# A stored order for 1,827 operations in the place of a list scheduler, in a complex linear attention with an expert layer

## The chip, the cores and the metric

One core of a Trainium2 chip runs the whole program. The metric is the device time of one execution in microseconds (us). Runs of the kernel before and of the changed kernel are compared on the same chip.

## The reference

The first half is a linear attention with a complex decay per channel, over 4 batches, 8 heads, 768 steps and 48 channels. The second half is an expert layer with 384 inputs and 2,048 hidden columns on all 3,072 tokens.

```python
mag = np.sqrt(a_re * a_re + a_im * a_im)
scale = np.minimum(mag, 0.999) / (mag + 1e-06)
a_re_n, a_im_n = (a_re * scale, a_im * scale)
for t in range(S):
    ar, ai = (a_re_n[:, :, t, :, None], a_im_n[:, :, t, :, None])
    new_re = ar * S_re - ai * S_im
    new_im = ar * S_im + ai * S_re
    kv = np.einsum('bhd,bhe->bhde', k[:, :, t], v[:, :, t])
    S_re, S_im = (new_re + kv, new_im)
    y[:, :, t] = np.einsum('bhd,bhde->bhe', q[:, :, t], S_re)
...
h = x @ w_in
g = h * (1.0 / (1.0 + np.exp(-1.702 * h)))
return (g @ w_out).astype(np.float32)
```

## The kernel before

The 3,072 tokens are cut into 12 units of 256 tokens (`u` 0 to 11). Each unit has two chunks of 128 tokens. Unit 0 is prepared in two halves of 128 tokens, so that the first matmuls can begin early.

`prepare` turns the decays into scaled and rotated queries and keys. It uses logarithms and exponentials on ScalarE (lines 569 to 581, one table), arctangent (line 589, another table), sine (lines 653 and 654, the table of the gate in all units but the first), and scans and products on VectorE. `remap` then moves `qr` and `qk` into the layout by heads, `qkh`, with five transfers from SyncE for each of the two (lines 676, 677, 679).

`attend` works on TensorE in four kinds of small pieces: the turning of keys (line 769), which ScalarE copies out to `kt` (line 772); the scores (line 714, 32 matmuls a piece), which VectorE multiplies by the mask into `pm` (line 718); the mix of scores, values and state (line 739), which ScalarE copies to `xhi` (line 748) and VectorE splits into `xlo` (line 752); and the update of the state (line 763). There is one PSUM tile for the scores, and one for the turned keys.

`moe` is the expert layer, over seven blocks of tokens: units 0 and 1 alone, in full fp32 (`whole`), and then five blocks of two units each, in three products of high and low halves. A hidden piece is line 819 (nine matmuls of 128x512 into `h_ps`, two buffers), the gate is line 832 on ScalarE (line 828 for the first two blocks), its split is lines 835 and 837 on VectorE, and a project piece is line 851 (nine matmuls, summed in three PSUM tiles `o_ps` over the block).

The weights arrive as 64-bit words. `convert` makes fp32 of them (lines 486 on ScalarE, 487, 490 and 493 on VectorE) and `split` makes the halves. Both lie in the first third of the program, beside the first units. Thirteen warm matmuls on data that are not used (line 661) run ahead of the first attention piece.

What sets the order is a planner. Every operation is an entry of `Plan` with its engine, an estimated duration, a rank, and the names of what it reads and writes. `Plan.order` ran a list scheduler forward and backward over the entries in many rounds, timed each candidate order with a model of the queues, and kept the best. Each engine then has the operations in the order so found, in one queue, and starts each when its inputs are there. Only the initial work stands outside of the plan: constants, the mask and the clearing of `qkh` (lines 393 to 412).

Of the kernel before, what the change touches and what calls it, by code (L numbers as in the profile page):

```python
# [21 lines left out]
P = 128  # L22
L = 128
HL = 64
QL = 32
NQ = L // QL
# [38 lines left out]
class Clock:  # L65


    def __init__(self):
        self.now, self.done, self.full = -1, 0.0, False

    def end(self, start, dur, work):
        t = start
        while dur > 1e-6:
            k = int(t / WINDOW + 1e-9)
            if k != self.now:
                self.full = k == self.now + 1 and self.done >= BUSY
                self.now, self.done = k, 0.0
            rate = 1.0 if self.full else 0.5
            step = min(dur, ((k + 1) * WINDOW - t) * rate)
            self.done += step * work  # L80
            dur -= step
            t += step / rate
        return t


def lag(a, b):
    return LAGS.get((a, b), LAG)


class Plan:  # L90
# [5 lines left out]
    def add(self, eng, dur, rank, fn, r=(), w=(), tab=None, name="", grp=None, work=1.0, kind=None):  # L96
# [10 lines left out]
        self.ops.append((eng, dur, rank, fn, deps, tab, name, grp, work))  # L107

    def link(self):
        self.after = [[] for _ in self.ops]  # L110
        for n, o in enumerate(self.ops):
            for d in o[4]:
                self.after[d].append(n)

    def groups(self):
        todo = {}
        for o in self.ops:
            if o[7] is not None:
                todo[o[7]] = todo.get(o[7], 0) + 1
        return todo  # L120

    def forward(self, rank, stay):

        ops, after = self.ops, self.after
        left = [len(o[4]) for o in ops]
        ready = [0.0] * len(ops)
        free = dict(FREE)
        wait = {e: [] for e in ENGINES}
        can = {e: [] for e in ENGINES}
        table, hw, dma, idle = None, 0.0, 0.0, 0.7  # L130
        todo, held = self.groups(), None
        clock = Clock()
        kinds, kind = self.kinds, "a"
        for n, k in enumerate(left):
            if not k:
                heapq.heappush(wait[ops[n][0]], (0.0, n))
        start = [0.0] * len(ops)
        done = 0
        while done < len(ops):
            best = None  # L140
            for e in ENGINES:
                while wait[e] and wait[e][0][0] <= free[e]:
                    n = heapq.heappop(wait[e])[1]
                    heapq.heappush(can[e], (rank[n], n))
                if can[e]:
                    s = free[e]
                elif wait[e]:
                    s = wait[e][0][0]
                else:
                    continue  # L150
                if best is None or s < best[0]:
                    best = (s, e)
            s, e = best
            if not can[e]:
                while wait[e] and wait[e][0][0] <= s:
                    n = heapq.heappop(wait[e])[1]
                    heapq.heappush(can[e], (rank[n], n))
            if e == "ACT":
                fit = [x for x in can[e] if ops[x[1]][5] in (None, table) or held in (None, ops[x[1]][7])]
                if not fit:  # L160
                    later = [free[x] for x in ENGINES if x != e and free[x] > s]
                    later += [wait[e][0][0]] if wait[e] else []
# [1051 lines left out]
```

## Time and profile before

| | us |
|---|---|
| median of 3 runs | 587.56 (585.82 to 588.19) |
| the profiled execution, its own time | 586.36 |
| its span | 584.6 |
| TensorE busy | 540.1 |
| VectorE busy | 470.1 |
| ScalarE busy | 275.6 |
| GpSimd busy | 27.4 |

The profiled execution lies 1.2 us under the median of the runs. Its span is what the profile shows from the first to the last instruction; 1.8 us of its time lie around the span. Busy time of TensorE counts overlapping matmuls once, and their ends are modelled.

### The profile page before, as it was taken

How to read it: one execution, taken by the hardware profiler on the slowest of the kernel's cores; microseconds unless marked ns; L12 is line 12 of the kernel's file. 1: busy time of each engine (PE TensorE's matmuls, PEld its weight loads, DVE VectorE, ACT ScalarE, POOL GpSimd, SP SyncE). 2: the span in 40 equal slices, each digit the busy share in tenths (PEclk: the TensorE clock that was granted, in tenths of full speed). 3: DMA queues.
4: the chain of work that ended last, by engine and by line, in shares of the span. 5: the costliest groups of instructions: out<-in, count | busy, mean ns of one | idle time of the engine just before them, and what ended most of it. 6: DMA issues, size and time to landing. Idle time of an engine off the chain costs nothing.

```text
span 584.6 us, 14786 instructions
## 1 busy us (share of the span) xinstructions
PE 540.1 (92%) x6236; PEld 445.1 (76%) x6236; DVE 470.1 (80%) x826; ACT 275.6 (47%) x428; POOL 27.4 (5%) x85
## 2 busy tenths in 40 slices
PE   0178999999999999999999999999999999999997
PEld 0166887887877878878888888878878888878885
DVE  6999889999899999888979789898775874654343
ACT  5975858885447355463543463553541221111110
POOL 7001000000101000000000000000000000000000
PEclk9998999999999999999999999999999999999999
DMA  8467983466455282681751762742962264232111
GB/s 323 138 193 304 275 259 117 82 193 116 164 137 166 44 169 72 116 267 51 138 181 44 148 214 69 135 171 69 185 192 73 66 119 82 85 127 56 36 46 56
DMA packets 30901, 80.06 MB, mean 137 GB/s; under 512 B 4208, under 2 KB 7024, under 8 KB 30832
## 3 DMA queue, kind: packets, MB, share of 16 engines
q1 hardware_dynamic: 30832, 79.09, 50.3%
q8 instruction: 49, 0.80, 0.6%
q14 instruction: 20, 0.16, 0.1%
HBM read 55.44 MB, written 4.72 MB: 103 GB/s over the span
## 4 chain that ended last, share of the span: by engine, by line
PE 66%; DVE 4%; issue 1%; ACT 1%; DMA 1%; DVEq 0%
PE o_ps L851 27%; PE h_ps L819 27%; PE x_ps L739 5%; PE p_ps L714 3%; PE kz_ps L769 2%; PE kz_ps L763 2%; DVE pm L718 1%; DMA raw_w<-in_w_in_dram 1%; DVE loU L511 0%; DVE qk L468 0%; DVE qr L468 0%; DVE gl L837 0%; DVE gh L835 0%; ACT kt L772 0%; DVE xlo L752 0%
## 5 line engine op out<-in xcount | busy, mean ns | idle before, releaser
L832 ACT ACTIVATE g<-h_ps 128x512 f32<-128x512 f32 x80 | 47.3, 597 | 161.3 <-PE h_ps L819 144.4
L851 PE MATMUL o_ps<-gh,hiU 128*128 128x512 f32 x240 | 96.5, 402 | 0.0
L819 PE MATMUL h_ps<-xhi,hiA 128*128 128x512 f32 x240 | 95.8, 399 | 0.6 <-ACT xhi L748 0.6
L851 PE MATMUL o_ps<-gl,hiU 128*128 128x512 f32 x240 | 93.8, 391 | 0.0
L819 PE MATMUL h_ps<-xlo,hiA 128*128 128x512 f32 x240 | 93.6, 390 | 0.1
L851 PE MATMUL o_ps<-gh,loU 128*128 128x512 f32 x240 | 93.6, 390 | 0.0
L819 PE MATMUL h_ps<-xhi,loA 128*128 128x512 f32 x240 | 93.6, 390 | 0.0
L835 DVE CAST gh<-g 128x512 fp32r<-128x512 f32 x80 | 33.8, 423 | 43.2 <-PE o_ps L851 39.3
L837 DVE TENSOR_TENSOR gl<-g,gh 128x512 fp32r<-128x512 f32 x80 | 55.2, 690 | 5.5
L772 ACT ACTIVATE kt<-kz_ps 128x224 f32<-128x224 f32 x80 | 28.3, 354 | 60.3 <-PE kz_ps L769 28.2
L819 PEld LDWEIGHTS h_ps<-xhi,hiA 128*128 128x128 f32 x240 | 45.0, 188 | 10.4 <-ACT xhi L748 0.9
L883 DVE TENSOR_REDUCE fit<-raw_w 128x1 f32<-128x256 f32 x96 | 37.8, 411 | 18.8 <-DMA raw_w<-in_w_out_dram 17.4
L851 PEld LDWEIGHTS o_ps<-gl,hiU 128*128 128x128 f32 x240 | 45.1, 188 | 10.2 <-DVE gl L837 0.6
L851 PEld LDWEIGHTS o_ps<-gh,hiU 128*128 128x128 f32 x240 | 45.1, 188 | 9.9 <-issue 1.0
L819 PEld LDWEIGHTS h_ps<-xhi,loA 128*128 128x128 f32 x240 | 45.1, 188 | 9.5
L819 PEld LDWEIGHTS h_ps<-xlo,hiA 128*128 128x128 f32 x240 | 45.1, 188 | 9.1 <-DVE xlo L752 0.4
L851 PEld LDWEIGHTS o_ps<-gh,loU 128*128 128x128 f32 x240 | 45.1, 188 | 8.4
L851 PE MATMUL o_ps<-g,valU 128*128 128x256 f32 x192 | 46.6, 383 | 1.6 <-issue 1.0
L819 PE MATMUL h_ps<-x,valA 128*128 128x256 f32 x192 | 47.7, 392 | 0.0
L468 DVE TENSOR_TENSOR qk<-qk,s 128x768 f32<-128x768 f32 (+1 forms) x52 | 45.3, 890 | 2.5 <-ACT s L654 1.8
L718 DVE TENSOR_TENSOR pm<-p_ps,mask 128x512 f32<-128x512 f32 x48 | 33.1, 690 | 15.7 <-PE p_ps L714 14.5
L1039 ACT ACT_TABLE_LOAD x35 | 44.9, 1283 | 1.4 <-PEq L1202 0.8
(92 smaller groups left out, 857.5 us busy)
## 6 DMA issues: line engine op xcount, KB each, us to landing
v<-in_v_dram SPq DMA_DIRECT2D x24, 416.0 KB, 3.9
ri<-in_a_dram SPq DMA_DIRECT2D x11, 768.0 KB, 5.2
qk<-in_qk_dram SPq DMA_DIRECT2D x11, 768.0 KB, 5.0
qkh<-qr SPq DMA_DIRECT2D x22, 288.6 KB, 5.8
qkh<-qk SPq DMA_DIRECT2D x22, 288.6 KB, 6.7
raw<-in_w_in_dram SPq DMA_DIRECT2D x8, 768.0 KB, 7.4
raw<-in_w_out_dram SPq DMA_DIRECT2D x8, 768.0 KB, 5.3
raw_w<-in_w_in_dram SPq DMA_DIRECT2D x24, 256.0 KB, 2.9
```

The source lines that it names most:

```text
L468: add(en, t, rank, lambda: e.tensor_tensor(out=out, in0=a, in1=b, op=alu), **kw)
L714: mm(p_ps[to : to + QL, j, lo:L], lhsT=at(h, 1, c)[:, lo : lo + QL], rhs=at(h, 0, c)[:, lo:L], start=True, stop=True)
L718: add("DVE", d_t(CW), rk(4 * c + hh), lambda hh=hh: dve.tensor_tensor(out=pm[hh], in0=p_ps, in1=mask, op=ALU.mult), r=["P"], w=[f"pm{hh}"])
L739: mm(x_ps[32 * j : 32 * j + 32, r, :], lhsT=lt, rhs=rt, start=n == 0, stop=n == len(steps) - 1)
L772: add("ACT", a_t(2 * KD) - 0.12, rk(4 * c + hh), lambda e=e: act(out=kt[0][:, 2 * e : 2 * e + 2, :], in_=k_ps, func=AF.Copy), r=["K"], w=[ ...
L819: mm(h_ps[hb][:, hs], lhsT=ww[:, r * T + f * P : r * T + (f + 1) * P], rhs=x[:, r, :], start=r + k == 0, stop=r == NR - 1 and k == len(ter ...
L832: add("ACT", a_t(N) - 0.15, rk(i + f / 2), lambda hb=hb, hs=hs: act(out=g32[hb][:, hs], in_=h_ps[hb][:, hs], func=AF.Silu, scale=SLOPE), r ...
L835: add("DVE", d_t(N, 2), rk(i + f / 2), lambda hb=hb, hs=hs: dve.tensor_copy(out=high.g(hb)[:, hs], in_=g32[hb][:, hs]), r=regs("g", kf), w ...
L837: add("DVE", d_t(N), rk(i + f / 2), lambda hb=hb, hs=hs: dve.tensor_tensor(out=glo[hb][:, hs], in0=g32[hb][:, hs], in1=high.g(hb)[:, hs].b ...
L851: mm(o_ps[m][:, 0:N], lhsT=y[:, f * DM + m * P : f * DM + (m + 1) * P], rhs=x[:, hs], start=i == 0 and f == 0 and k == 0, stop=i == NP - 1 ...
L883: add("DVE", d_t(CK), rk + 2, lambda x=x, op=op: dve.tensor_reduce(out=f_w[:, x, n : n + 1], in_=weights.looked_at()[:, :, 1], op=op, axis ...
L1039: nc.scalar.preload_act_table_set(o[5])
```

## The change

The list scheduler and its model go, with all their constants. `Plan.order` now reads a stored list of 1,827 numbers and asserts that it holds every operation once and each behind those that it depends on. The list was found by annealed moves inside the engines' queues. The operations themselves are the 1,819 of before and eight new ones. The eight are `clear`: the second `qkh` buffer was cleared by one GpSimd instruction of 4,104 columns ahead of the plan, and is now cleared by eight of 513 columns in the plan, which wait for the first `rc` of unit 0. The mask is made with six copies in place of twelve. The argument `size` on the entries is not read any more when the kernel is built.

```diff
     def order(self):
-
-        self.link()
-        best = None
-        for part, stay in PARTS:
-            rank = [o[2] for o in self.ops]
-            for k in range(ROUNDS):
-                start, end = self.forward(rank, stay)
-                order = sorted(range(len(start)), key=lambda n: start[n])
-                cost = sum(w * self.time(order, x) for x, w in COST)
-                if best is None or cost < best[0]:
-                    best = (cost, order)
-                late = self.backward(start)
-                rank = [x + part * (end - y - x) for x, y in zip(rank, late)]
-        return best[1]
+        coded = base64.b85decode("".join(ORDER))
+        order = struct.unpack(f">{len(coded) // 2}H", coded)
+        place = {n: i for i, n in enumerate(order)}
+        assert len(place) == len(self.ops) == len(order)
+        assert all(place[d] < place[n] for n, o in enumerate(self.ops) for d in o[4])
+        return order
...
+CLEAR = 513
+ORDER = (
+    "0D=He0002L0A&CV0I2{90G9xR0E7Th0EGaC08#*l08;>q0Ehro00IC30FM9z0FVGx0E_@u09gP80F3}z0FD4%0FwY)0A2uz09*iJ0Ez%t0FeM#"
...
-    for j in range(1, NQ):
-        for x in range(NQ):
-            y = (x + j) % NQ
-            nc.gpsimd.tensor_copy(out=mask[y * QL : (y + 1) * QL, j, :], in_=mask[x * QL : (x + 1) * QL, 0, :])
+    for x in range(NQ):
+        y = (x + 1) % NQ
+        nc.gpsimd.tensor_copy(out=mask[y * QL : (y + 1) * QL, 1, :], in_=mask[x * QL : (x + 1) * QL, 0, :])
+    for x in range(2):
+        nc.gpsimd.tensor_copy(out=mask[(1 - x) * HL : (2 - x) * HL, 2:NQ, :], in_=mask[x * HL : (x + 1) * HL, 0:2, :])
     half = H * T
     nc.vector.memset(qkh[0][:, 0:half], 0.0)
     nc.gpsimd.memset(qkh[0][:, half:], 0.0)
-    nc.gpsimd.memset(qkh[1], 0.0)
...
+    def clear(n):
+        part = qkh[1][:, n * CLEAR : min((n + 1) * CLEAR, H * (2 * T + 1))]
+        add("POOL", 0.45, 14 + 0.5 * n, lambda: pool.memset(part, 0.0), r=["rc0"], w=[f"H1.{c}.{x}" for c in range(2) for x in range(2)])
+
     for n, units in enumerate(BLOCKS):
+        if n == 1:
+            for k in range(-(-H * (2 * T + 1) // CLEAR)):
+                clear(k)
         for u in units:
             prepare(u)
             attend(u)
```

Three places show how the queues change. Lines 511, 536, 560 and 566 of the changed kernel are lines 714, 739, 763 and 769 of before; 616 and 648 are 819 and 851; 843 is 1039; 629 is 832; 366 and 367 are 569 and 570.

The first place is TensorE's queue at the second chunk of unit 8, before: two score pieces follow each other with only one turning of keys between them.

```order
L714 MATMUL p_ps<-qkh_76 32x128 x4
L714 MATMUL p_ps<-qkh_76 32x96 x4
L714 MATMUL p_ps<-qkh_76 32x64 x4
L714 MATMUL p_ps<-qkh_76 32x32 x4
L769 MATMUL kz_ps<-ident,qkh_76 128x112 x2
L714 MATMUL p_ps<-qkh_75 32x128 x4
L714 MATMUL p_ps<-qkh_75 32x96 x4
L714 MATMUL p_ps<-qkh_75 32x64 x4
```

The same score piece of chunk 1 of unit 8 now has a hidden piece of nine matmuls ahead of it.

```order
L566 MATMUL kz_ps<-ident,qkh_76 128x112 x2
L616 MATMUL h_ps_106<-xhi_2905,hiA_884 128x512
L616 MATMUL h_ps_106<-xlo_91,hiA_884 128x512
L616 MATMUL h_ps_106<-xhi_2905,loA_1860 128x512
L616 MATMUL h_ps_106<-xhi_2905,hiA_884 128x512
L616 MATMUL h_ps_106<-xlo_91,hiA_884 128x512
L616 MATMUL h_ps_106<-xhi_2905,loA_1860 128x512
L616 MATMUL h_ps_106<-xhi_2905,hiA_884 128x512
L616 MATMUL h_ps_106<-xlo_91,hiA_884 128x512
L616 MATMUL h_ps_106<-xhi_2905,loA_1860 128x512
L511 MATMUL p_ps<-qkh_76 32x128 x4
```

An update of the state and a project piece stand ahead of this turning, so that two pieces of nine matmuls now lie between the two score pieces of the chunk.

The second place is TensorE's queue where the last block of the expert layer begins, before: the first hidden piece stands right behind the last mix of unit 11.

```order
L739 MATMUL x_ps<-pm_95,v_87 32x128 x2
L739 MATMUL x_ps<-pm_96,v_87 32x128 x2
L739 MATMUL x_ps<-qkh_75,st_94 32x128 x4
L819 MATMUL h_ps_105<-xhi_4732,hiA_358 128x512
L819 MATMUL h_ps_105<-xlo_91,hiA_358 128x512
L819 MATMUL h_ps_105<-xhi_4732,loA_730 128x512
```

Now a project piece of the block before stands between that mix and the hidden piece.

```order
L536 MATMUL x_ps<-qkh_75,st_94 32x128 x4
L648 MATMUL o_ps_107<-gh_1724,hiU_1231 128x512
L648 MATMUL o_ps_107<-gh_1724,loU_2230 128x512
L648 MATMUL o_ps_107<-gl_100,hiU_1231 128x512
L648 MATMUL o_ps_108<-gh_1724,hiU_1231 128x512
L648 MATMUL o_ps_108<-gh_1724,loU_2230 128x512
L648 MATMUL o_ps_108<-gl_100,hiU_1231 128x512
L648 MATMUL o_ps_109<-gh_1724,hiU_1231 128x512
L648 MATMUL o_ps_109<-gh_1724,loU_2230 128x512
L648 MATMUL o_ps_109<-gl_100,hiU_1231 128x512
L616 MATMUL h_ps_105<-xhi_4754,hiA_1014 128x512
```

A project piece has moved in between the last mix of a unit and the first hidden piece of the next block; this is so at all five blocks of two units.

The third place is ScalarE's queue where unit 6 is prepared beside the expert block of units 2 and 3, before: all logarithms and exponentials of the unit (lines 569 to 581) stand between two table loads, and no gate among them.

```order
L1039 ACT_TABLE_LOAD
L569 ACTIVATE s_84<-s_84,small 128x3x256
L772 ACTIVATE kt_97<-kz_ps 128x224
L748 ACTIVATE xhi_1913<-x_ps 128x3x128
L570 ACTIVATE s_84<-s_84 128x3x256
L772 ACTIVATE kt_97<-kz_ps 128x224
L580 ACTIVATE s_80<-s_84,small 128x3x256
L581 ACTIVATE s_80<-s_80 128x3x256
L578 ACTIVATE s_81<-s_81,small 128x3x256
L579 ACTIVATE s_81<-s_81 128x3x256
L1039 ACT_TABLE_LOAD
```

Now, where unit 7 is prepared beside that same block, the logarithm and its exponential have a table load of their own, and the sine of unit 6 and the gates follow with another.

```order
L843 ACT_TABLE_LOAD
L366 ACTIVATE s_84<-s_84,small 128x3x256
L367 ACTIVATE s_84<-s_84 128x3x256
L843 ACT_TABLE_LOAD
L451 ACTIVATE s_85<-s_85 128x3x256
L629 ACTIVATE g_99<-h_ps_106 128x512
L569 ACTIVATE kt_97<-kz_ps 128x224
L629 ACTIVATE g_98<-h_ps_105 128x512
```

Gates have moved in between the parts of a unit's group of logarithms, with a table load at each change. In the whole queue the executed loads go from 35 to 59.

## Rows read from the trace of the kernel before

**Rows 1.** The page's part on engines, first line: busy us, share, instructions.

```profile
PE 540.1 (92%) x6236; PEld 445.1 (76%) x6236; DVE 470.1 (80%) x826; ACT 275.6 (47%) x428; POOL 27.4 (5%) x85
```

**Rows 2.** Busy time by stage: stretch, us, engines, granted clock, DMA share, GB/s.

```profile
0.00:49.93 49.93, 17.64 (x361) 14.40 (x361) 43.76 (x86) 35.85 (x58) 15.43 (x35) 1.00 0.68 241
49.93:140.00 90.07, 88.21 (x884) 75.43 (x882) 85.52 (x126) 66.37 (x104) 2.33 (x10) 0.98 0.66 185
140.00:300.00 160.00, 155.77 (x2025) 127.21 (x2017) 145.61 (x244) 85.81 (x127) 6.74 (x25) 1.00 0.55 136
300.00:514.00 214.00, 212.20 (x2690) 174.06 (x2688) 166.11 (x306) 77.90 (x125) 2.87 (x15) 1.00 0.47 118
514.00:580.40 66.40, 66.17 (x290) 53.96 (x290) 28.40 (x64) 9.62 (x17) 0.00 (x0) 1.00 0.19 57
```

**Rows 3.** Timeline of the opening: start, us, engine, line, operation, idle before.

```profile
8.91 3.52 POOL L410 MEMSET qkh<- 128x4104 f32 x1
...
9.99 2.86 DVE L487 TENSOR_SCALAR valA<-raw 128x768 int32<-128x768 int32 x1 [1.48 <-DMA raw<-in_w_in_dram]
...
26.60 7.44 PE L661 MATMUL h_ps<-qk,ident 128*128 128x256 f32 x26 [26.60 <-DVE qk L468]
...
28.33 1.17 SPq L676 DMA_DIRECT2D qkh<-qk  x2
...
31.62 0.55 DVE L487 TENSOR_SCALAR valA<-raw 128x768 int32<-128x768 int32 x1
...
33.88 0.36 PE L769 MATMUL kz_ps<-ident,qkh 112*128 112x112 f32 x2
...
35.99 0.34 ACT L772 ACTIVATE kt<-kz_ps 128x224 f32<-128x224 f32 x1
```

**Rows 4.** Timeline, end of unit 0's attention and the first hidden piece.

```profile
44.41 0.75 DVE L718 TENSOR_TENSOR pm<-p_ps,mask 128x512 f32<-128x512 f32 x1
...
46.78 2.08 DVE L628 TENSOR_TENSOR_SCAN s<-small,s 128x256 f32<-128x256 f32 x3
...
49.40 0.35 PE L763 MATMUL kz_ps<-v,kt 128*16 128x48 f32 x12 [2.41 <-issue]
...
49.93 7.04 PE L819 MATMUL h_ps<-x,valA 128*128 128x256 f32 x24
```

**Rows 5.** Busy time by stretch just behind it; the granted clock stands third from the end.

```profile
50.00:52.00 2.00, 2.00 (x7) 1.63 (x7) 2.00 (x4) 1.81 (x3) 0.00 (x0) 0.58 1.03 419
52.00:54.00 2.00, 2.00 (x6) 1.59 (x6) 2.00 (x4) 1.37 (x2) 0.00 (x0) 0.57 0.29 113
```

**Rows 6.** Timeline of TensorE, five of its waits; the bracket is idle before.

```profile
146.11 1.13 PE L851 MATMUL o_ps<-g,valU 128*128 128x256 f32 x4 [1.04 <-issue]
...
183.48 1.00 PE L714 MATMUL p_ps<-qkh 128*32 128x128 f32 x30 [0.84 <-DVE pm L718]
...
218.97 0.41 PE L769 MATMUL kz_ps<-ident,qkh 112*128 112x112 f32 x2 [1.13 <-ACT kt L772]
...
387.56 0.77 PE L714 MATMUL p_ps<-qkh 128*32 128x128 f32 x30 [0.49 <-DVE pm L718]
...
514.12 0.50 PE L819 MATMUL h_ps<-xhi,hiA 128*128 128x512 f32 x1 [0.61 <-ACT xhi L748]
```

**Rows 7.** Timeline of TensorE where a hidden piece ends and a mix follows.

```profile
295.11 0.39 PE L819 MATMUL h_ps<-xlo,hiA 128*128 128x512 f32 x1
295.33 0.39 PE L819 MATMUL h_ps<-xhi,loA 128*128 128x512 f32 x1
295.65 0.86 PE L739 MATMUL x_ps<-pm,v 128*32 128x128 f32 x24
```

**Rows 8.** Groups on ScalarE: count, busy us, mean ns, idle before, what ended it.

```profile
L832 ACT ACTIVATE g<-h_ps 128x512 f32<-128x512 f32 x80 | 47.3, 597 | 161.3 <-PE h_ps L819 144.4 <-DVE gl L837 7.8 <-issue 5.6
L1039 ACT ACT_TABLE_LOAD x35 | 44.9, 1283 | 1.4 <-PEq L1202 0.8
```

More of the change, by code (lines that the diff above doesn't have):

```diff
@@ L1 @@
-import heapq
+import base64
 import math
+import struct
 from contextlib import ExitStack
@@ L62 @@
 SLOPE = 1.702
[L65 to L87, printed above, removed]
 class Plan:
@@ L94, in __init__, with add @@
         self.ops, self.wrote, self.read, self.kinds = [], {}, {}, []
-    def add(self, eng, dur, rank, fn, r=(), w=(), tab=None, name="", grp=None, work=1.0, kind=None):
+    def add(self, eng, dur, rank, fn, r=(), w=(), tab=None, name="", grp=None, work=1.0, kind=None, size=1):
         n = len(self.ops)
@@ L282, in time @@
-    def time(self, order, load):
-        ops = self.ops
-        free = dict(FREE)
-        ends = [0.0] * len(ops)
-        table, hw, dma, idle = None, 0.0, 0.0, 0.7
-        clock = Clock()
-        kinds, kind = self.kinds, "a"
-        for n in order:
-            e, dur = ops[n][0], ops[n][1]
-            s = max([free[e]] + [ends[d] + lag(ops[d][0], e) for d in ops[n][4]])
-            if e == "SP":
-                free[e] = s + 0.06 + 0.65 * (ops[n][8] - 1)
-                hw = max(hw, s + 0.06) + 0.47 * ops[n][8]
-                dma = max(dma, hw + 0.6) + dur
-                ends[n] = dma + 0.9
-                continue
-            if ops[n][5] not in (None, table):
-                dur += max(0.0, load - (s - idle))
-                table = ops[n][5]
-            if e == "PE":
-                dur += CHANGE[kind, kinds[n]]
-                kind = kinds[n]
-            free[e] = ends[n] = clock.end(s, dur, ops[n][8]) if e == "PE" else s + dur
-            if e == "ACT":
-                idle = s + dur
-        return max(ends)
@@ L715, in scores @@
                                start=True, stop=True)
-                add("PE", 0.6, rk(4 * c + hh), scores, r=hk[c], w=["P"], name=f"P{u}.{c}.{hh}", work=0.97, kind="m")
+                add("PE", 0.6, rk(4 * c + hh), scores, r=hk[c], w=["P"], name=f"P{u}.{c}.{hh}", work=0.97, kind="m", size=4 * NQ * NQ + 1)
                 add("DVE", d_t(CW), rk(4 * c + hh), lambda hh=hh: dve.tensor_tensor(
@@ L823, in moe @@
                 for rs in PIECES:
-                    add("PE", len(rs) * terms_of * columns, rk(i + f / 2 - 0.5), lambda rs=rs, hidden=hidden: hidden(rs), r=xk + cols, w=regs("h", kf), name=f"H{n}.{i}", work=0.975, kind="a")
+                    add("PE", len(rs) * terms_of * columns, rk(i + f / 2 - 0.5), lambda rs=rs, hidden=hidden: hidden(rs), r=xk + cols, w=regs("h", kf), name=f"H{n}.{i}", work=0.975, kind="a", size=len(rs) * (4 if whole else 6) + 1)
             for f in range(2):
@@ L861, in moe @@
                     r=[k for y in (("gh",) if whole else ("gh", "gz")) for f in fs for k in regs(y, at(f)[2])] + cols, w=[f"o{m}" for m in ms],
-                    name=f"O{n}.{i}", work=0.975, kind="a")
+                    name=f"O{n}.{i}", work=0.975, kind="a", size=len(fs) * len(ms) * (4 if whole else 6) + 1)
         spent = [f"x{y}{b}.{c}" for y in "hl" for c in range(4)]
```

234 lines of the change are left out of this document (47 added, 187 removed).

## The prediction

> **What bounds the kernel now.** I read the page's line of engines first: TensorE is busy for 540.1 us of the span of 584.6, VectorE for 470.1, ScalarE for 275.6 [rows 1]. TensorE bounds, so the next question is where it does not work. The stages answer it [rows 2]. Up to 49.93 us, where the first hidden piece of the expert layer starts [rows 4], TensorE is busy for 17.64 us: this opening is bounded by VectorE (43.76 us busy of 49.93) and by what it feeds. From there to 580.4 us TensorE idles for 1.86, 4.23, 1.80 and 0.23 us in the four stages (stretch less busy), 8.12 us in all. In that second part a new order can only win these 8.12 us, a stretch at half clock, and the small cost of changing from one kind of matmul to another; the matmuls themselves stay.
>
> The idle 8.12 us come in a few large waits, and I looked each up. Five are in [rows 6]. The waits at 183.48 and 387.56 us are of a kind that comes at least twice more: a score piece stands right behind the one before it, and must wait until VectorE has read the single PSUM tile of scores. The wait at 218.97 us is a turning of keys behind ScalarE's copy of the last one. The wait at 514.12 us is the first hidden piece of the last block behind the copy of the mix. The wait at 146.11 us is of another sort: it begins in the middle of a piece and ends by "issue", so neither data nor a buffer was late; the queue had no instruction ready. The largest of this sort lies in the opening, 2.41 us in the middle of a state update [rows 4]. Behind it the first hidden pieces run at a granted clock of 0.58 and 0.57 for the next four microseconds [rows 5], nearly half of 2.4 GHz: some 4 x 0.42 = 1.7 us lost.
>
> **The change part by part.**
>
> *GpSimd's clearing.* One clearing of 3.52 us, from 8.91 to 12.43 us, overlaps a VectorE conversion that takes 2.86 us; the same conversion takes 0.55 us elsewhere [rows 3]. The conversion ends 0.42 us behind the clearing, so I read it as held up by it: 2.31 us of VectorE in the opening. The clearing now comes in eight pieces, 3.52 x 513 / 4,104 = 0.44 us each, so one conversion can be held up by that much at most. The pieces stand in the plan behind unit 0's first `rc`, and the buffer is first written by unit 2, so nothing waits for them. The fewer mask copies are hidden: nothing reads the mask before unit 0's scores.
>
> *The opening's order.* The second half of the decay work of unit 0 is now first, and one weight is converted between, with its load moved ahead of the queries' loads on SyncE. In time for the first attention piece it matters that SyncE's second five transfers, those from `qk`, start at 28.33 us [rows 3], though their input was complete when the warm matmuls started, at 26.60 us: SyncE was still issuing the five from `qr`. In the new VectorE queue the two products for `qr` stand well ahead of the last product for `qk`, with scans and products between, so the first five will be out when the second can start. That is worth up to 28.33 - 26.60 = 1.7 us; and five of the thirteen warm matmuls, which end just before the first turning at 33.88 us, are moved behind it. ScalarE's first copy of keys, at 35.99 us, is 2 us behind the turning that it copies [rows 3]; in the new queue it stands earlier against unit 1's logarithms. So the first attention pieces come 2 to 3 us earlier. But then a loss: in the new VectorE queue unit 1's angle scan (three instructions, 2.08 us, [rows 4]) stands ahead of the last mask product of unit 0, where before only a decay product and one conversion step stood, and three more conversion steps stand ahead of the mask product before that. I take 1.2 us for the opening: from 0 (all given back by VectorE, which has hardly a gap there) to 2.4 (the 2.41 us wait for instructions gone, and nothing else).
>
> *The half clock.* It came behind the wait for instructions. Three warm matmuls now stand between the second chunk's pieces, but a wait for the last mask product stays. I take half of 1.7 us, 0.8; bounds 0 and 1.7.
>
> *Waits in the second part.* I went through the new TensorE queue for the four kinds of wait. No score piece stands behind another any more without either an expert piece or mixes of the chunk between them; nine matmuls in steps of 0.22 to 0.23 us [rows 7] are 2.0 us, and the mask product that must fit in between takes 0.75 [rows 4]. Before every block of two units a project piece stands between the last mix and the first hidden piece, 2.0 us against the 0.61 that it idled. The turning of 218.97 us has three expert pieces ahead of it. So these waits go: the five of [rows 6] less that for instructions are 3.07 us, and two more of the score kind, which I take at 0.4 each since the two shown are 0.84 and 0.49, make it 3.9. The waits for instructions stand behind dense runs of small matmuls, which expert pieces now break up more evenly. I take another 1.2 us there, a little more than the one of 1.04, and leave 3.0 of the 8.12 as they are: a gain of 5.1. Bounds: 2 (VectorE's waits come back elsewhere) and 8.1.
>
> *Changes of kind.* A matmul step of 0.22 us inside a hidden piece becomes 0.32 us where a mix follows [rows 7]: 0.1 us for leaving, and I bound the entry by the same. TensorE's queue changes between expert and attention pieces 150 times before, and 140 times now: 1.0 us. Of the returns to expert work, 32 came directly from scores, mixes or updates and 15 do now; the others go by way of a turning of two matmuls. I take 1.5 us; bounds 0 and 2.5.
>
> *ScalarE's tables.* 24 more loads at 1.283 us are 30.8 us of ScalarE [rows 8]. It idles 161.3 us ahead of the 80 large gates alone, nearly all for TensorE [rows 8], and a load has no input to wait for, so it runs in such an idle stretch. I take nothing for it; if the cover is gone, a load delays the gate and then the project piece by up to 1.28 us. The Trainium skill speaks against this part: "ScalarE: Activation LUTs", section "What ACT_TABLE_LOAD costs", counts a drain of 1.38 us with each load, 2.66 us for every switch. By that figure the 24 loads would be an estimated 64 us of ScalarE, still less than its idle time. The trace of before agrees with the load's 1.283 us and shows 1.4 us of idle ahead of all 35 together, which leaves no room for a drain there.
>
> *The sum.* 1.2 + 0.8 + 5.1 + 1.5 = 8.6 us against the profiled execution's 586.36, so 577.8. The median of the runs is 1.2 us above that execution, and I set the forecast against the median: **579.0 us**, 1.5% faster. The likeliest case's own range is from 573 (nearly all of the idle time and the clock) to 584.
>
> **The rivals.** *VectorE keeps the time.* In the stage from 49.93 to 140 us VectorE is busy for 85.52 of 90.07 us, and from 140 to 300 us for 145.61 of 160 [rows 2]. If the gates' splits and weight halves are late whatever TensorE's order, waits move from score pieces to expert pieces. For it: only 4.6 us of VectorE's time are free in the first of these stages. Against it: by 300 us another 14.4 are, and the clearing gives 2.3 back. Then only the last 284 us gain (2 us of idle time) and about 1 us of changes: 584 to 587. *The order has nothing to give*, since it does not fit the chip and each of its wins is paid elsewhere: also here.
>
> *More is won.* The waits for instructions and the half clock go altogether, and the opening gains 2.4: 2.4 + 1.7 + 8.1 + 2.5 = 14.7, so 573 or less.
>
> *Slower, by ScalarE's tables.* In the stretches where a unit's logarithms are cut by gates, a gate has two loads, 2.57 us, and the logarithms' part between them ahead of it. If TensorE has fewer than two expert pieces of other work between that gate's hidden piece and its project piece, it waits. It decides from 8.6 / 1.283 = 7 exposed loads on; with all in twelve places exposed it is 15.4 us: 579 + 15.4 = 594. Against it: in the new queue I find a project piece only rarely less than two expert pieces behind its hidden piece. For it: it is the one thing of which the change adds much. The skill's rule to batch work by table set ("ScalarE: Activation LUTs", section "Table sets: the hidden batching unit") would make this rival the case.
>
> **How the numbers follow.** The forecast's case has 0.60, more won 0.10, VectorE or nothing to give 0.20, slower 0.10. What a measurement of this kernel tells from no change is about half a per cent, 584.6 to 590.5. The second rival lies across its lower edge, a quarter of it faster, and a little of the forecast's own case falls short of it too. So faster 0.74, within 0.17, slower 0.09. The range leaves out the far parts of the first and last cases: 570.5 to 588.
>
> **What the profile after would show.** Right: the conversion of line 487 near 9 us takes about 0.6 us; the first hidden piece starts between 47.5 and 50; no granted clock near 0.6 behind it; TensorE idles some 3 us from there on; 59 table loads, with the gates' idle time still mostly for TensorE. Wrong: waits of TensorE's expert pieces for `g`, `gl` or `lo`, which would be VectorE or ScalarE late; or a first hidden piece later than 51 us.

## The result, and the profile after

The changed kernel takes 579.19 us (median of 4 runs, 578.89 to 579.99); the kernel before took 587.88 in the runs beside it (4 runs, 585.82 to 589.58). The ratio is 0.9856, with a 95% interval of 0.9822 to 0.9889: faster by 1.4%. The forecast was 579.0. The profiled execution took 579.99 us, span 578.3, against 586.36 and 584.6.

The page of the changed kernel, its part on engines, and the group of table loads:

```profile
PE 535.9 (93%) x6236; PEld 442.3 (76%) x6236; DVE 462.3 (80%) x826; ACT 301.0 (52%) x452; POOL 29.8 (5%) x86
...
L843 ACT ACT_TABLE_LOAD x59 | 75.7, 1283 | 1.8 <-PEq L1006 0.8
```

Busy time by stage of the changed kernel, columns as in [rows 2]. The first stage now ends at the first hidden piece, 47.61 us, and the last with TensorE:

```profile
0.00:47.61 47.61, 17.97 (x361) 13.99 (x361) 43.33 (x87) 35.54 (x58) 9.78 (x30) 1.00 0.70 245
47.61:140.00 92.39, 88.20 (x965) 74.69 (x958) 87.55 (x130) 74.28 (x111) 11.19 (x19) 1.00 0.66 182
140.00:300.00 160.00, 158.15 (x2106) 130.69 (x2109) 145.18 (x245) 92.62 (x134) 5.45 (x23) 1.00 0.54 139
300.00:514.00 214.00, 213.90 (x2570) 175.85 (x2563) 161.02 (x307) 91.09 (x138) 3.34 (x15) 1.00 0.45 118
514.00:571.60 57.60, 57.59 (x255) 47.05 (x253) 24.52 (x58) 7.45 (x13) 0.00 (x0) 1.00 0.19 58
```

The span's 6.3 us have three parts. The first hidden piece is 2.3 us earlier (49.93 to 47.61). From there to the last matmul it is 523.99 us instead of 530.47, 6.5 less. But the span ends 6.7 us behind the last matmul (578.3 - 571.6), where before it ended 4.2 behind it (584.6 - 580.4): 2.5 us are given back.

What TensorE waits for, all stages together (total us, times, longest):

```profile
PE h_ps L616 <- ACT g L625: 4.6, 5, 1.5
PE x_ps L536 <- DVE pm L515: 1.8, 2, 1.2
PE kz_ps L560 <- DVE st L579: 1.6, 1, 1.6
PE p_ps L511 <- issue: 1.0, 1, 1.0
```

The waits of score pieces for the mask product, of the turning and of the last block's hidden piece [rows 6] are gone. The wait "by issue" of 1.04 us at 146.11 is gone too, but one of 0.95 us now stands in a score piece at 155.59 (the last line). The first line is new: hidden pieces that wait for a gate of the whole blocks. Here are TensorE's large waits in order of time:

```profile
39.04 0.53 PE L560 MATMUL kz_ps<-v,kt 128*32 128x48 f32 x32 [1.60 <-DVE st L579]
...
45.35 0.43 PE L536 MATMUL x_ps<-pm,v 128*32 128x128 f32 x8 [1.25 <-DVE pm L515]
...
60.71 1.56 PE L616 MATMUL h_ps<-x,valA 128*128 128x256 f32 x6 [0.97 <-ACT g L625]
...
106.46 2.86 PE L616 MATMUL h_ps<-x,valA 128*128 128x256 f32 x12 [0.62 <-ACT g L625]
...
110.79 1.56 PE L616 MATMUL h_ps<-x,valA 128*128 128x256 f32 x6 [1.48 <-ACT g L625]
...
118.60 1.56 PE L616 MATMUL h_ps<-x,valA 128*128 128x256 f32 x6 [0.86 <-ACT g L625]
...
146.36 1.56 PE L616 MATMUL h_ps<-x,valA 128*128 128x256 f32 x6 [0.68 <-ACT g L625]
...
155.59 0.34 PE L511 MATMUL p_ps<-qkh 128*32 128x64 f32 x10 [0.95 <-issue]
```

The timeline of ScalarE ahead of the wait at 118.60 shows why the gate is late: it stands behind an arctangent, a weight half that nobody needs soon, and a table load. A table load of 1.28 us stands right ahead of three of the five late gates (at 104.73, 116.87 and 144.63 us).

```profile
110.36 0.38 ACT L625 ACTIVATE g<-h_ps 128x256 f32<-128x256 f32 x1
...
113.98 1.28 ACT L843 ACT_TABLE_LOAD   x1
115.28 0.84 ACT L386 ACTIVATE s<-s 128x768 f32<-128x768 f32 x1
116.03 0.83 ACT L303 ACTIVATE hiU<-valU 128x768 fp32r<-128x768 f32 x1
116.87 1.28 ACT L843 ACT_TABLE_LOAD   x1
118.17 0.38 ACT L625 ACTIVATE g<-h_ps 128x256 f32<-128x256 f32 x1
```

And the end. The last tile leaves VectorE at 572.27, and only then do all three stores of 256 KB start (last two lines). Before (first two lines) they were issued over 3.08 us from 578.39 on, two of them ahead of the last tile, which VectorE began at 580.42.

```profile
578.39 3.08 SPq L870 DMA_DIRECT2D out_dram<-o  x3
...
580.42 0.69 DVE L866 TENSOR_SCALAR o<-o_ps 128x512 f32<-128x512 f32 x1 [0.67 <-PE o_ps L851]
...
571.58 0.69 DVE L663 TENSOR_SCALAR o<-o_ps 128x512 f32<-128x512 f32 x1 [0.67 <-PE o_ps L648]
...
572.30 1.31 SPq L667 DMA_DIRECT2D out_dram<-o  x3
```

In SyncE's stored order the third tile's store stands ahead of the second's and the first's; before, they stood in the order in which the tiles become ready.

### The profile page after: what moved, and what is told of

Its sections match the earlier page's. It is cut to its first block, busy times and chain, and to the rows that moved or that the text cites. A ratio compares the mean times of both kernels' runs of the same rounds, so it can differ in the third digit from the quotient of the medians.

```text
span 578.3 us, 14771 instructions
## 1 busy us (share of the span) xinstructions
PE 535.9 (93%) x6236; PEld 442.3 (76%) x6236; DVE 462.3 (80%) x826; ACT 301.0 (52%) x452; POOL 29.8 (5%) x86
## 4 chain that ended last, share of the span: by engine, by line
PE 75%; ACT 3%; DMA 1%; DVE 1%; issue 0%; SPq 0%; ACTq 0%
PE o_ps L648 30%; PE h_ps L616 30%; PE x_ps L536 6%; PE p_ps L511 4%; PE kz_ps L566 3%; PE kz_ps L560 2%; DMA v<-in_v_dram 1%; ACT L843 1%; ACT hiA L303 0%; ACT g L625 0%; DVE s L391 0%; ACT hiU L303 0%; ACT s L375 0%; DVE s L438 0%; ACT s L386 0%
## 5 line engine op out<-in xcount | busy, mean ns | idle before, releaser
L616 PE MATMUL h_ps<-x,valA 128*128 128x256 f32 x192 | 45.6, 384 | 4.6 <-ACT g L625 4.6
```

The source lines that it names most:

```text
L616: mm(h_ps[hb][:, hs], lhsT=ww[:, r * T + f * P : r * T + (f + 1) * P], rhs=x[:, r, :], start=r + k == 0, stop=r == NR - 1 and k == len(ter ...
```

## The experiments

Each run is timed beside the kernel before on the same chip. Medians of the kernel before differ by up to 1.5 us between chips, so effects below are also read as differences of ratios, 0.001 of which is 0.59 us. The intervals are 2 to 5 us wide; where those of two runs overlap, the time alone does not separate them, and the reading rests on the traces, one profiled execution of each kernel.

| run | median us | ratio to before | 95% interval |
|---|---|---|---|
| the change | 579.19 | 0.9856 | 0.9822 to 0.9889 |
| stores_in_turn | 576.79 | 0.9795 | 0.9759 to 0.9830 |
| gates_first | 578.09 | 0.9819 | 0.9780 to 0.9859 |
| masks_first | 580.19 | 0.9849 | 0.9814 to 0.9884 |
| one_clear | 580.84 | 0.9861 | 0.9825 to 0.9896 |
| order_of_before | 586.90 | 0.9980 | 0.9953 to 1.0007 |
| opening_of_before | 582.93 | 0.9909 | 0.9890 to 0.9927 |
| rest_of_before | 584.27 | 0.9923 | 0.9903 to 0.9943 |
| loads_added | 592.21 | 1.0070 | 1.0050 to 1.0090 |
| halves_together | 574.96 | 0.9780 | 0.9744 to 0.9816 |
| copy_first | 580.67 | 0.9869 | 0.9831 to 0.9906 |
| no_late_warm | 581.09 | 0.9875 | 0.9840 to 0.9911 |
| all_together | 573.26 | 0.9755 | 0.9726 to 0.9784 |

Moves are written as pairs: in the stored order, the first operation goes right ahead of the second. Four lines are added for it, so line numbers of those kernels are four higher.

```diff
-        order = struct.unpack(f">{len(coded) // 2}H", coded)
+        order = list(struct.unpack(f">{len(coded) // 2}H", coded))
+        for n, m in AHEAD:
+            order.remove(n)
+            order.insert(order.index(m), n)
```

**The stores.** Operations 1656 to 1658 are the stores of the three last tiles.

```diff
+AHEAD = ((1657, 1658), (1656, 1657),)
```

> The changed order on all engines, only the last three stores of SyncE in the order in which their tiles become ready (first, second, third; in the changed order third, second, first). Theory, the queue of stores: in the changed kernel all three start at 572.30 us, behind the last tile, and the last byte lands some 4 us later; in the kernel before they start at 578.39, some 0.9 us and some 2.7 us behind that, and the tail behind the last matmul is 4.3 us instead of 6.8. So the last matmul stays at 571.5, the span shrinks by 2.0 to 2.5 us, and the median falls from 579.2 to about 576.8. Rival, the end is set by something else (the four instruction packets near 574.8 us, the closing of the program): span and median stay within 0.5 us.

The stores start from 569.47 on, the last alone behind the last tile:

```profile
571.13 0.69 DVE L667 TENSOR_SCALAR o<-o_ps 128x512 f32<-128x512 f32 x1 [0.68 <-PE o_ps L652]
...
571.85 0.33 SPq L671 DMA_DIRECT2D out_dram<-o  x1
```

The span is 575.3: from the last tile's start on VectorE to the end it is 4.2 us, against 6.7 (578.3 - 571.58). The first theory holds, by place and size; the median is the one expected. All six times (576.32 to 578.19) lie below the four of the changed kernel.

**The two halves of the order.** Three kernels carry another stored list. In the first, every queue is in the order of before, so that only the short clearings (and the fewer mask copies) are left; in the second only what stands ahead of the first hidden piece is in the order of before; in the third all but that. Line numbers of these kernels are one lower.

```diff
 ORDER = (
-    "0D=He0002L0A&CV0I2{90G9xR0E7Th0EGaC08#*l08;>q0Ehro00IC30FM9z0FVGx0E_@u09gP80F3}z0FD4%0FwY)0A2uz09*iJ0Ez%t0FeM#"
+    "08jve0A&D|00005015!901p7a08s!^0D}Ni0E7Tk0EGZm0EPfo09gQ609^oD0A2tB09XKr0AB!z09ycy09*ix0AT=(0Ez&Q0Am1+0Ac`;0FeNW0A"
...
```

> The order of the kernel before in every queue, with the clearing in eight pieces: the first two behind unit 0's decay sums near 14 us, the others where the changed order has them. So of the whole change only GpSimd's clearing is left. Theory of the prediction: the conversion that took 2.86 us takes under 1 us, VectorE is 2.3 us earlier in the opening, and some 1 to 2.3 us of it reach the first hidden piece (47.6 to 49.0 instead of 49.93) and the end: median 585.6 to 587 against 587.9. Rival: other things set the opening (inputs, SyncE's transfers), the first hidden piece stays within 0.5 us of 49.93 and the median within 0.7 us of before.

> The changed kernel, but the operations that its order lists ahead of the first hidden piece stand among themselves in the order of before; all others as changed. Theory, the new opening is worth what the traces show (first hidden piece 49.93 to 47.61, half clock 1.7 us): median up by 2.3 to 4.0 us from the changed kernel, to 581.5 to 583.2, with the wait for instructions and the low granted clock back behind it. Rival, VectorE's total sets the early stage, so that the opening's gain is largely waited away until 140 us: median up by less than 1 us.

> The other half: the operations that the changed order lists ahead of the first hidden piece stand as changed, all others in the order of before (with its order of the last stores). Theory, the two parts add up: the opening gives 2.3 to 4.0 us of the 8.7, and the rest is as before: median 583.9 to 585.6, the waits of TensorE for mask products at the scores are back, no wait of an expert piece for a gate over 0.5 us, tail 4.3 us. Rival, the early stage eats the gain: median above 586.5.

With the order of before, the conversion now takes 0.56 us, but a wait for instructions of 2.96 us stands in the same state update as before [rows 4]; the first hidden piece starts at 48.98:

```profile
9.08 0.56 DVE L283 TENSOR_SCALAR valA<-raw 128x768 int32<-128x768 int32 x1 [0.60 <-DMA raw<-in_w_in_dram]
...
48.11 0.51 PE L559 MATMUL kz_ps<-v,kt 128*16 128x48 f32 x12 [2.96 <-issue]
```

The first hidden piece is 0.95 us earlier than before, but so was the conversion's start: its weights came 0.91 us earlier in this execution (9.08 against 9.99), which the clearing does not set. The second kernel has the same old opening with short clearings; its conversion took 0.56 us too, its weights came at 10.25, and its first hidden piece starts at 49.61. From the conversion's start to the first hidden piece it is 39.94 us in the kernel before, 39.90 and 39.36 in these two. So of the 2.31 us that the conversion lost, between 0 and 0.6 us reached the first hidden piece; part of it is lost again where a tensor_scalar of three columns meets the new pieces (1.11 us at 15.11 instead of 0.18). In the median, where the interval takes in 1, it can't be told from nothing. The old opening under the new rest has the same wait, at 49.08 (2.65 us), and the low clock behind it (third column from the end):

```profile
50.00:52.00 2.00, 2.00 (x7) 1.53 (x6) 2.00 (x4) 1.28 (x1) 0.00 (x0) 0.50 0.04 8
52.00:54.00 2.00, 2.00 (x8) 1.64 (x7) 2.00 (x4) 1.44 (x3) 0.00 (x0) 0.65 0.86 258
```

By medians the opening is worth 586.90 - 584.27 = 2.6 us beside the old rest and 582.93 - 579.19 = 3.7 beside the new; the rest is worth 4.0 or 5.1, with the stores' 2.5 already taken off. By ratios the opening is 3.4 or 3.1 and the rest 4.2 or 3.9, and the opening alone and the rest alone make 7.6 together, against 7.3 for both at once: the two parts add up within the noise, as the theories said. One detail of the third expectation missed: one hidden piece waits 1.3 us for a gate there too.

The third kernel also separates the rest's order from the clock: it has the opening of the changed kernel, and the granted clock is 1.00 from the first hidden piece to the last matmul in both. From there on TensorE is busy for 520.98 us with the old rest (first line) and for 517.84 with the new (second line), 3.1 less.

```profile
47.00:578.39 531.39, 520.98 (x5884) 429.43 (x5876) 425.36 (x739) 240.51 (x371) 14.92 (x57) 1.00 0.50 128
...
47.61:571.60 523.99, 517.84 (x5884) 428.27 (x5876) 418.27 (x739) 265.43 (x395) 19.98 (x57) 1.00 0.48 129
```

**The clearing.** The first piece clears everything, the other seven nothing.

```diff
-        part = qkh[1][:, n * CLEAR : min((n + 1) * CLEAR, H * (2 * T + 1))]
-        add("POOL", 0.45, 14 + 0.5 * n, lambda: pool.memset(part, 0.0),
+        add("POOL", 0.45, 14 + 0.5 * n, lambda: pool.memset(qkh[1], 0.0) if n == 0 else None,
```

> The changed order, but the first of the eight clearing pieces clears the whole buffer at once and the other seven do nothing. Theory of the prediction, a long clearing holds VectorE up by 2.31 us: whatever VectorE does near 14.4 us is held up by about 2 us, the opening is bounded by VectorE, and the first hidden piece comes near 49.6 instead of 47.6 us; median up by about 2 us to 581.2. Rival, the clearing's length is worth nothing to the end: VectorE loses the time, but the chain to the first hidden piece has slack for it or the expert layer's waits take it up: median within 0.7 us of 579.2.

The median is 1.7 us up, but by ratio nothing is (0.9861 against 0.9856), and in the profiled execution, the fastest of its six at 577.82, VectorE is not held up and the first hidden piece starts at 46.23:

```profile
13.54 3.55 POOL L720 MEMSET qkh<- 128x4104 f32 x1
13.66 0.18 DVE L400 RECIPROCAL small<-small 128x3 f32<-128x3 f32 x1
...
13.85 0.56 DVE L265 TENSOR_TENSOR s<-ri,s 128x384 f32<-128x384 f32 x1
14.33 1.23 DVE L407 TENSOR_TENSOR_SCAN s<-s,small,s 128x128 f32<-128x128 f32 x3
```

Both theories as I wrote them miss: VectorE loses next to nothing. What stands beside the clearing matters, not its length alone. In the changed kernel a tensor_scalar of three columns beside two pieces takes 1.10 us, and 0.16 us here where the clearing begins.

**The gates on ScalarE.**

```diff
+AHEAD = ((226, 418), (357, 362), (408, 362), (368, 426), (387, 695), (393, 432),)
```

> The changed order, with five gates of whole blocks 0 and 1 moved in ScalarE's queue ahead of work that nobody waits for (copies of weight halves, and once a copy of weights and a gate with later input). Theory, ScalarE's queue: TensorE's five waits for a gate (4.6 us in all, longest 1.64) go, the last matmul comes 3 to 4.6 us earlier (567 to 568.5), the median is 574.6 to 576.2. Rival, VectorE keeps the time (85 of 90 us busy in this stage before the change): other waits of TensorE between 50 and 150 us grow by as much, the last matmul moves by less than 1 us, the median by less than 1.

By ratio 2.2 us are gained, by the median 1.1, and the intervals overlap; the first theory expects 3.0 to 4.6. Four of the five waits go; that of 118.60 stays and grows to 1.60, and a new one of 1.75 stands at a project piece, behind a conversion on ScalarE that waits 1.39 us for its weights:

```profile
67.16 1.56 PE L652 MATMUL o_ps<-g,valU 128*128 128x256 f32 x6 [1.75 <-ACT g L629]
116.54 1.56 PE L620 MATMUL h_ps<-x,valA 128*128 128x256 f32 x6 [1.60 <-ACT g L629]
```

**The halves.** Looked at piece by piece, the waiting piece of 118.60 should have been free: the plan's names make it wait only for the gate of its own 256 columns of `h_ps`, done at 110.36 + 0.38, yet it starts 0.05 us behind the end of the gate at 118.17, which reads the other 256 columns. In the built program a hidden piece waits for the gate of either half; the plan keeps the halves apart (`regs("h", kf)`), and the stored order often puts something between them. This kernel has the stores in turn as well.

```diff
+AHEAD = ((1657, 1658), (1656, 1657), (225, 230), (360, 355), (367, 358),)
```

> The stores in turn as in the run of that name, and three hidden pieces of whole blocks 0 and 1 moved in TensorE's queue right behind the other half of the same piece, so that both halves of one PSUM tile of hidden values are written before a gate reads either. Theory, halves: in the program a hidden piece waits for the gate that reads the other half of its PSUM tile, which the plan's own list of dependences does not hold, so its order put a gate between the halves; without that, the waits at 60.7, 106.5, 110.8 and 118.6 us (3.85 of 4.6 us) go and the median is 573 to 574 against the 576.8 of the stores alone. Rival, ScalarE's queue: the gates are late for whoever asks, so that project pieces wait for g instead; median within 1 us of 576.8.

1.8 us are gained by the median over the stores alone (0.9 by ratio, with overlapping intervals), and in the traces the last matmul starts 2.8 us earlier (571.02 to 568.19) with the same start of the warm matmuls. The waits at 106.46 and 118.60 are gone. That of 60.71 is now at a project piece, and that of 110.79 stays, both behind gates late on ScalarE:

```profile
67.13 1.56 PE L652 MATMUL o_ps<-g,valU 128*128 128x256 f32 x6 [1.61 <-ACT g L629]
...
109.34 2.86 PE L620 MATMUL h_ps<-x,valA 128*128 128x256 f32 x12 [1.48 <-ACT g L629]
```

Both theories have a part. By the plan's names all five pieces wait for the gate of the other half (the fifth, at 146.36 us, was left as it was); two of these waits go when the halves stand together, the other three need ScalarE's order as well.

**All together.** The same, and gates ahead of what need not be early on ScalarE.

```diff
+AHEAD = ((1657, 1658), (1656, 1657), (225, 230), (360, 355), (367, 358), (226, 418), (227, 56), (232, 56), (357, 362), (387, 695), (393, 432),)
```

> The stores in turn and the halves together, and five gates moved in ScalarE's queue: two ahead of a conversion that waits for its weights (that pair ended the wait of 1.61 us at 67.13 us in the run with the halves), one ahead of a gate with later input (1.48 us at 109.34), two ahead of a table load or a half's copy (0.68 us at 143.78), and one ahead of two copies of halves near 58 us. Theory, these three waits of 3.77 us are only a matter of ScalarE's order: last matmul 2.5 to 3.8 us earlier than 568.19, median 571.2 to 572.5 against 574.96. Rival, VectorE or the weights' loads are behind the gates: other waits come between 60 and 150 us, median within 1 us of 574.96.

The three waits are gone, and in the stage of the second line above TensorE is busy for 92.10 of 92.39 us:

```profile
47.61:140.00 92.39, 92.10 (x1053) 78.76 (x1052) 91.17 (x140) 78.14 (x118) 8.29 (x20) 1.00 0.67 182
```

The last matmul is 3.2 us earlier (565.02), 0.7 of it a start that was earlier in this execution. The median, 573.26, gains 1.7 over the last kernel (1.5 by ratio, with overlapping intervals): short of the theory's 2.5, beyond the rival's 1. At 0.9755 it beats the changed kernel (0.9856) by 1.0%, with intervals apart.

**The opening.** Two products ahead of two conversion steps on VectorE, and the angle's scan behind the mask product; in the second kernel also ScalarE's copy `xhi` ahead of unit 1's angles.

```diff
+AHEAD = ((183, 9), (173, 13), (296, 297),)
...
+AHEAD = ((183, 9), (173, 13), (296, 27), (297, 204),)
```

> The changed order, with two products that TensorE waits for in the opening moved ahead of two conversion steps on VectorE, and the scan of unit 1's angle moved behind the last mask product of unit 0. Theory, the order on VectorE sets the opening: TensorE's waits at 39.04 (1.60 us) and 45.35 (1.25 us) go, the first hidden piece starts 2.0 to 2.8 us earlier than 47.61, and so does all behind it: median 576.4 to 577.2. Rival, VectorE keeps the time: the first hidden piece comes earlier, but the moved conversions and unit 1's decay work are late for what follows, waits between 47 and 140 us grow by as much, last matmul and median within 0.7 us of the changed kernel.

> The run on the mask products again (two products ahead of two conversion steps, the angle's scan behind the last mask product), and on ScalarE the last copy of the mix ahead of the part of unit 1's angles that waits for that scan. Theory, ScalarE's copy was what ate the gain there: the first hidden piece starts near 46.5 us instead of 47.62, and what follows comes 0.7 to 1.1 us earlier than in the changed kernel: median 578.1 to 578.5. Rival, VectorE keeps the time: the first hidden piece comes at 46.5, but the waits between 50 and 140 us grow by the same amount, the last matmul stays within 0.4 us of 571.5 and the median within 0.7 of 579.2.

In the first kernel the wait of 1.60 is gone and that of 1.25 is 0.39, but the first hidden piece does not move, as ScalarE's copy stands behind the angles:

```profile
47.62 4.15 PE L620 MATMUL h_ps<-x,valA 128*128 128x256 f32 x18 [0.93 <-ACT x L549]
```

In the second it starts at 46.01, 1.6 us earlier, 0.6 of it an earlier start of the warm matmuls. But three waits of 3.0 us follow before 70 us, where the changed kernel has the one of 0.97 and one of 0.3; the last matmul is no earlier (it starts at 572.23, in the changed kernel at 571.47):

```profile
56.76 2.86 PE L620 MATMUL h_ps<-x,valA 128*128 128x256 f32 x12 [0.73 <-ACT g L629]
...
61.12 2.86 PE L620 MATMUL h_ps<-x,valA 128*128 128x256 f32 x12 [1.50 <-ACT g L629]
...
68.61 1.56 PE L652 MATMUL o_ps<-g,valU 128*128 128x256 f32 x6 [0.75 <-ACT g L629]
```

The theory fails: an earlier opening is worth nothing there, and the median is 1.5 us up (0.8 by ratio, with overlapping intervals), a little past the rival's 0.7. That it is VectorE's load and not ScalarE's queue behind it, these runs do not settle, since the waits end at gates.

**The late warm matmuls.** The five between the first pieces are left out; their result is not used.

```diff
-                    add("PE", 0.43, -WARM + k, kind="a", size=5, fn=lambda k=k, dst=dst: mm(
+                    add("PE", 0.43, -WARM + k, kind="a", size=5, fn=lambda k=k, dst=dst: None if k > 7 else mm(
```

> The changed order without the five warm matmuls that stand between unit 0's attention pieces (the first eight stay); they feed nothing. Theory, they keep the clock: with the waits of 1.60 and 1.25 us the granted clock falls in the opening, behind 47 us it is near 0.6 for some 4 us, and about 1.7 us are lost: median near 581. Rival, the clock fell before only because of the wait for instructions of 2.4 us and more: the granted clock behind the first hidden piece stays 1.00, and the median stays within 0.7 us of 579.2.

The clock falls, though earlier than I expected, in the attention pieces, and by the expert layer it is back:

```profile
34.00:36.00 2.00, 0.97 (x23) 0.93 (x26) 2.00 (x4) 1.70 (x3) 0.00 (x0) 0.85 0.69 168
36.00:38.00 2.00, 1.40 (x26) 0.98 (x20) 2.00 (x3) 0.55 (x2) 0.00 (x0) 0.50 0.51 66
...
42.00:44.00 2.00, 1.51 (x48) 1.21 (x41) 1.76 (x4) 2.00 (x5) 0.10 (x1) 0.94 1.01 393
...
50.25 0.27 PE L560 MATMUL kz_ps<-v,kt 128*16 128x48 f32 x4 [1.62 <-issue]
```

The last row is from its timeline: a wait by issue in the state update of the second chunk is back too (1.62 us). Behind the first hidden piece the granted clock is 1.00 (50 to 54 us), as the rival says, in spite of that wait. So the late warm matmuls hold the clock up in the attention pieces; that they do it behind the first hidden piece, this run does not show. The first hidden piece comes at 50.44, 2.8 us later, the last matmul 2.4 later (573.86). The median is up 1.9 us, the size that the theory expected, but by another way; by ratio it is 1.1, which the intervals don't separate.

**More table loads.** A pair ahead of each of 24 gates. At eight of them one load stood already, so there are 99 loads, 40 more than in the changed kernel and not 48, and 51.3 us more of ScalarE.

```diff
+AGAIN = (838, 848, 858, 868, 878, 888, 898, 908, 1091, 1101, 1111, 1121, 1131, 1141, 1151, 1161, 1332, 1342, 1352, 1362, 1372, 1382, 1392, 1402)
...
+            if n in AGAIN:
+                nc.scalar.preload_act_table_set(LOGS)
+                cur = LOGS
```

> The changed order, with two table loads more ahead of each of 24 gates (the first of each pair in the blocks of units 4 to 9): 107 loads instead of 59, 61.6 us more of ScalarE between 250 and 500 us. Theory of the prediction, a load runs in idle time of ScalarE and a project piece seldom stands close enough behind: median within 1 us of the changed kernel's 579.2, ScalarE's busy time up by 62 us. Rival, exposed loads: each pair delays its gate and the project piece by 1.3 to 2.6 us, at twelve gates or more, so 15 to 60 us slower. The Trainium skill, ScalarE: Activation LUTs, section What ACT_TABLE_LOAD costs, would count 2.66 us for each load with its drain, an estimated 128 us of ScalarE for the 48; the idle time ahead of the gates would show the drains as 1.38 us ahead of each load.

13.0 us slower, so the theory of the prediction falls and the rival's lower end is nearly met. L844 are the 24 added loads, L847 all others. TensorE, which idled 0.10 us between 250 and 400 us, idles 9.1 there, and runs at a granted clock of 0.97 in the first 50:

```profile
250.00:300.00 50.00, 45.84 (x403) 36.84 (x402) 40.12 (x72) 31.59 (x39) 1.97 (x10) 0.97 0.50 127
300.00:350.00 50.00, 47.38 (x618) 38.65 (x618) 38.82 (x71) 34.70 (x43) 0.98 (x5) 1.00 0.43 117
350.00:400.00 50.00, 47.68 (x513) 38.16 (x515) 39.44 (x74) 37.60 (x45) 1.28 (x5) 1.00 0.48 131
...
L847 ACT ACT_TABLE_LOAD x75 | 96.2, 1283 | 1.8 <-PEq L1010 0.8
L844 ACT ACT_TABLE_LOAD x24 | 30.8, 1283 | 0.4
```

That is 0.33 us for a load, a quarter of its 1.283: most run in idle time, some don't. The drain of 1.38 us that the Trainium skill counts with each load ("ScalarE: Activation LUTs", section "What ACT_TABLE_LOAD costs") does not show: the 99 loads have 2.2 us of idle time ahead of them in all. This run agrees with the Trainium skill's rule to batch work by table set ("ScalarE: Activation LUTs", section "Table sets: the hidden batching unit"); what the change's own 24 more loads cost, no run shows.

## Why the prediction was right, and where it was not

The gain forecast at 8.6 us is 8.7 by the medians, and 6.4 by the two profiled executions, of which the one of before is that of the sum and the one of after is the slowest of its four. That the forecast's 579.0 lies so near to 579.19 is in part luck: its terms are off by up to 3.1 us, both ways, and a loss of 2.5 us was not in it. By the prediction's own signs the account is mixed: the conversion, the first hidden piece, the clock and the 59 loads came as said, but TensorE idles 6.15 us instead of "some 3", and its hidden pieces wait for `g`, which stood there as a sign of being wrong. By the terms, with the profiled executions:

- **The opening**, taken at 1.2, is 2.3 at the first hidden piece, near the upper bound of 2.4; 0.4 of it is there at the first warm matmul (26.60 to 26.20). In six other executions with the same opening the first hidden piece starts at 46.14 to 47.07, so 2.3 is at the low end. Its parts came as said: first turning 1.65 us earlier (33.88 to 32.23), the wait for instructions gone, and the last mask product late behind unit 1's scan (1.25 us at 45.35). That the first conversion no longer meets the clearing is right, but its worth was over-read: at most 0.6 of its 2.31 us reached the first hidden piece in the old order.
- **The half clock**, taken at 0.8, is the whole 1.7: the granted clock is 1.00 between 50 and 54 us. The three kernels with the old opening have the low clock behind their wait by issue of over 2 us (2.41, 2.96 and 2.65), and no kernel with another opening has it there; whether the wait or the places of the warm matmuls decide, no run separates. The bound of 0 rested on the wait for the last mask product; that wait came (1.25 us) and did not bring the low clock.
- **Changes of kind**, taken at 1.5. TensorE's busy time from the first hidden piece on falls from 522.35 to 517.84 us with the same matmuls: 4.5. Less 1.7 for the clock, 2.8 are left, a little over the bound of 2.5. The kernel with the old rest behind the new opening gives 3.1 for it, at full clock. So the saving belongs to the new order behind the opening; that all of it is changes of kind is still a reading.
- **The waits**, taken at 5.1, are only 2.0: idle time in this part goes from 8.12 to 6.15 us. The old waits for data and buffers went as predicted, and more of them than were counted. The 1.2 us for waits for instructions did not come: the wait of 1.04 us went and one of 0.95 came. The step that failed is that nothing new would come, in "leave 3.0 of the 8.12 as they are": 4.6 us of new waits for gates came. The prediction had priced late gates only as a rival ("Slower, by ScalarE's tables"), and only at project pieces. They came at hidden pieces, through the two halves of a PSUM tile and through a few gates behind work that can wait.
- **The tail** was not a term at all. It lost 2.5 us, since SyncE's last three stores are turned round. The prediction read SyncE's queue for the opening, not for the end.
- **ScalarE's tables** "at nothing": what the 24 loads cost by themselves is not shown. The reason given, that a load has no input to wait for, does not make it free: 40 at other places cost 13.0 us, and a load stands right ahead of three of the five late gates.

So 5.6 us of the predicted 8.6 were lost to two things not foreseen, the new waits (3.1) and the stores (2.5); the opening, the clock and the changes of kind, each taken low, brought 3.3 more than said: 6.3, the span's difference. Of the rivals, "VectorE keeps the time" has the right size in one place: what the opening gains beyond the change is waited away by 70 us. That VectorE is the cause there is not shown, since those waits end at gates.

## What to carry to other kernels

When a stored order or a planner takes the place of another, read every engine's queue to its last entry, the DMA queue too: three stores in turned order behind the last tile cost 2.5 us, about as much as the first hidden piece was moved forward (2.3). A planner's order is as good as its list of dependences; where the profile shows a wait that the plan doesn't know (here for the other half of a PSUM tile), put the two writers together or give the plan the dependence. Ahead of a gate, look at what stands in its engine's queue that nobody waits for yet.

## What the runs showed of the hardware

In these traces some VectorE instructions are held up beside a GpSimd clearing and others are not. Beside one of 3.52 us a tensor_scalar of 128x768 took 2.86 us instead of 0.55 [rows 3], and 0.56 where the clearing was moved away; beside one of 3.55 us products and scans took what they take elsewhere (0.56 and 1.23 us).

The wait "by issue" came in the update of the state of unit 0's second chunk in each kernel that had no warm matmuls between the attention pieces (2.41, 2.96 and 2.65 us with all thirteen ahead, 1.62 with eight), and in none with five of them in between. The prediction reads such a wait as a queue without a ready instruction; the profile shows only that TensorE waited for nothing that it records, and the cause stays open.

The start varies: in the executions profiled, the first warm matmul started between 24.78 and 26.60 us, and among kernels with the same opening between 24.79 and 26.20. In the changed kernel VectorE's first conversion waited 0.92 us for its weights; with the stores in turn, which leave the opening as it is, it did not (it starts at 7.65 instead of 8.59).
